# Softmax tiles copied into the split-operand type ahead of their transposes, in an LSH attention with two expert layers

## The chip, the core and the metric

The kernel runs on one core of a Trainium2 chip. The core has five engines with instruction streams of their own: PE (TensorE, matrix products; PEld are its weight loads), DVE (VectorE), ACT (ScalarE), POOL (GpSimd) and SP (SyncE, which here only issues DMAs). They wait for each other through semaphores. Each takes its own instructions in the order in which they stand. The metric is the device time of one execution in microseconds, as the median of three runs.

## The reference

Attention with hashed buckets over 2 batches, 8 heads, 768 positions and 64 dimensions: a query sees only the keys whose six projection signs are the same as its own. Two layers with a gate follow, 512 to 2048 to 512, over the 1536 tokens. All arrays are float32.

```python
q_bits = (np.einsum('bhsd,dk->bhsk', q, proj) > 0).astype(np.int64)
k_bits = (np.einsum('bhsd,dk->bhsk', k, proj) > 0).astype(np.int64)
...
mask = q_bucket[:, :, :, None] == k_bucket[:, :, None, :]
scores = scale * np.matmul(q, k.transpose(0, 1, 3, 2))
scores = np.where(mask, scores, -1000000000.0)
scores = scores - np.max(scores, axis=-1, keepdims=True)
attn = np.exp(scores)
attn = attn / (np.sum(attn, axis=-1, keepdims=True) + 1e-09)
return np.matmul(attn, v).astype(np.float32)
...
g = h * np.tanh(sp)        # layer 1, sp = softplus(h), h = x @ w_in
return (g @ w_out).astype(np.float32)
...
g = h - np.tanh(h)         # layer 2
return (g @ w_out).astype(np.float32)
```

## The kernel before

**Types.** A float32 value is split into a high and a low part, both held in fp32r, the type in which PE multiplies; a product is then two or three matmuls (high by high, high by low, low by high). Names that end in h and l are such parts. ACT or POOL makes the high part by a copy into fp32r, DVE or POOL the low part by a subtraction.

**Attention.** The eight pairs of heads (two heads share a pair, `g` counts pairs, `h` the head in it) run one after the other. For a pair, `load` fetches q, k and v; `halves_split` splits q and k in halves of 384 positions; `piece` takes the projection signs; `stack` copies the parts into four stacked operands a, b, c and d by eight DMAs per head (`b<-kh` twice, `a<-qh`, `a<-ql`, `d<-kl`, `c<-qh`, `d<-z`, `c<-z`). Then the queries go in tiles of 128, three tiles to a half, two halves to a head. `scores` (L566) makes one tile: four matmuls (L582, L583) into PSUM, a clamp on DVE that also takes the row's extreme (L586), and Exp on ACT (L609) into the tile p with the row sums beside it. `chunk` (L631) works on a half: for each of its six column blocks PE transposes the three p tiles (L643, three transposes per chunk, 576 in all), the 128x384 result is split into ph and pl, and a later `product` (L617) multiplies both with the values (L622, L623). For most chunks ACT copies and DVE subtracts (L659, L662); for the "pooled" ones of `POOL_C` ACT copies to f (L651) and POOL does both parts (L375, L655). `gather` (L669) joins the halves of the output; `inverse` (L681) adds, inverts and transposes the row sums and spreads them over the partitions by way of DRAM (four stores, two loads); `finish` (L710) multiplies and splits the result into xh and xl.

**Layers.** From about 235 us on the two layers run on PE with products by blocks (L1023 to L1025, L1100, L1101, L1113, L1338). They start from xh and xl and are not touched by the change.

**What sets the order.** Nothing is issued where the code stands. `op` records each operation with an engine, a cost and a key (a due time); `Plan.order` then plays the recorded operations through, picks for each engine the one that can start first (the lower key where several can), with costs and latencies from the table of constants at the head of the file, and emits the instructions in that order. So a change of the constants moves instructions on every engine. Each tile name has a ring of buffers: p has six (`P_BUFS`), and a new tile waits until the one whose buffer it takes has been read for the last time. All DMAs but a few at the start are issued by SP, in one queue.

## Time and profile before

| | |
|---|---|
| median of 3 runs | 741.01 us (741.01 to 741.36) |
| profiled execution | 740.89 us, span 739.1 us from the first to the last instruction |
| busy over the span | PE 98%, PEld 91%, DVE 87%, ACT 72%, POOL 24% |
| stretch of 60 to 220 us (attention) | PE 159.85 of 160 us, ACT 155.31, DVE 148.24, POOL 133.85, DMA share 0.66 |
| granted clock | 1.00 in every stretch of the attention, 0.999 over the span |

Averages over the span mix the attention, in which all engines work, with the layers, in which POOL has nothing to do. So the stretches are read apart. A matmul's busy time is modelled to its end, and matmuls overlap: a transpose is shown with 272 ns, though transposes start 109 ns apart. A busy PE is therefore not yet a full one; what a matmul costs is read from the distance between starts.

### The profile page before, as it was taken

How to read it: one execution, taken by the hardware profiler on the slowest of the kernel's cores; microseconds unless marked ns; L12 is line 12 of the kernel's file. 1: busy time of each engine (PE TensorE's matmuls, PEld its weight loads, DVE VectorE, ACT ScalarE, POOL GpSimd, SP SyncE). 2: the span in 40 equal slices, each digit the busy share in tenths (PEclk: the TensorE clock that was granted, in tenths of full speed). 3: DMA queues.
4: the chain of work that ended last, by engine and by line, in shares of the span. 5: the costliest groups of instructions: out<-in, count | busy, mean ns of one | idle time of the engine just before them, and what ended most of it. 6: DMA issues, size and time to landing. Idle time of an engine off the chain costs nothing.

```text
span 739.1 us, 13094 instructions
## 1 busy us (share of the span) xinstructions
PE 727.7 (98%) x4382; PEld 673.6 (91%) x4382; DVE 643.8 (87%) x1372; ACT 529.7 (72%) x1140; POOL 179.7 (24%) x224
## 2 busy tenths in 40 slices
PE   7999999999999999999999999999999999999998
PEld 4889999999999999999999999998998899999997
DVE  6988998998999999999898899789898775767893
ACT  6989999999997866767676676666565445466660
POOL 5677987988961000000000000000000000000000
PEclk9999999999999999999999999999999999999999
DMA  7775775785562655545655567999986786735621
GB/s 215 184 200 130 204 201 129 204 211 126 156 175 88 231 197 168 172 156 179 204 181 186 185 232 247 330 330 329 350 295 251 270 278 232 244 144 186 222 87 64
DMA packets 59390, 150.96 MB, mean 204 GB/s; under 512 B 7990, under 2 KB 20406, under 8 KB 59324
## 3 DMA queue, kind: packets, MB, share of 16 engines
q1 hardware_dynamic: 58892, 149.65, 63.9%
q8 instruction: 34, 0.56, 0.3%
q10 hardware_dynamic: 432, 0.49, 0.2%
q14 instruction: 32, 0.26, 0.1%
HBM read 88.18 MB, written 43.04 MB: 178 GB/s over the span
## 4 chain that ended last, share of the span: by engine, by line
PE 93%; DVE 2%; DMA 2%; ACT 2%; issue 1%; POOL 0%; ACTq 0%; SPq 0%; DVEq 0%; POOLq 0%
PE pt L1023 11%; PE pt L1025 11%; PE pt L1024 11%; PE pt L643 8%; PE pt L1101 6%; PE pt L1113 6%; PE s L1100 6%; PE pt L1100 6%; PE pt L1338 5%; PE s L582 4%; PE pt L622 4%; PE pt L623 4%; PE s L583 4%; PE s L1338 3%; PE s L1113 3%; DVE p L586 1%
## 5 line engine op out<-in xcount | busy, mean ns | idle before, releaser
L1023 PE MATMUL pt<-xh,a 128*128 128x384 f32 x288 | 96.7, 336 | 0.0
L1025 PE MATMUL pt<-xh,a 128*128 128x384 f32 x288 | 96.7, 336 | 0.0
L1024 PE MATMUL pt<-xl,a 128*128 128x384 f32 x288 | 96.6, 335 | 0.0
L586 DVE TENSOR_SCALAR_CACHE_REDUCE p<-s 128x768 f32<-128x768 f32 x93 | 88.2, 948 | 7.6 <-PE s L583 5.7
L609 ACT ACTIVATE p<-p,mn 128x768 f32<-128x768 f32 x96 | 90.7, 945 | 3.1 <-DVE p L586 2.0
L662 DVE TENSOR_TENSOR pl<-pt,ph 128x384 fp32r<-128x384 f32 x148 | 78.5, 546 | 8.6 <-ACT ph L659 7.6
L643 PE MATMUL pt<-cst,p 128*128 128x128 f32 x576 | 83.8, 272 | 1.1 <-DVE pl L662 1.1
L643 PEld LDWEIGHTS pt<-cst,p 128*128 128x128 f32 x576 | 69.5, 140 | 6.1 <-DVE pl L662 1.4
L659 ACT CAST ph<-pt 128x384 fp32r<-128x384 f32 x148 | 68.8, 484 | 5.2 <-PE pt L622 3.1
L1101 PE MATMUL pt<-gh,o 128*128 128x256 f32 x256 | 71.7, 280 | 0.0
L622 PE MATMUL pt<-ph,vt 128*128 128x384 f32 x192 | 70.4, 367 | 0.3 <-ACT f L651 0.2
L582 PE MATMUL s<-b,a 128*128 128x512 f32 (+1 forms) x186 | 68.2, 367 | 1.1 <-DVE p L586 0.7
L623 PE MATMUL pt<-pl,vt 128*128 128x384 f32 x192 | 64.9, 338 | 0.4 <-DVE pl L662 0.4
L583 PE MATMUL s<-d,c 77*128 77x512 f32 (+3 forms) x186 | 59.3, 340 | 0.6 <-ACT raw L846 0.6
L802 DVE TENSOR_TENSOR gl<-pl,gh 128x384 fp32r<-128x384 f32 x96 | 52.4, 551 | 6.5 <-ACT gh L1047 6.5
L1023 PEld LDWEIGHTS pt<-xh,a 128*128 128x128 f32 x288 | 54.1, 188 | 3.3 <-ACT pl L1042 0.2
L1024 PEld LDWEIGHTS pt<-xl,a 128*128 128x128 f32 x288 | 54.1, 188 | 1.3
L1025 PEld LDWEIGHTS pt<-xh,a 128*128 128x128 f32 x288 | 54.1, 188 | 0.1
L1047 ACT CAST gh<-pl 128x384 fp32r<-128x384 f32 x96 | 48.7, 514 | 2.1 <-DVE pl L802 1.1
L1101 PEld LDWEIGHTS pt<-gh,o 128*128 128x128 f32 x256 | 48.3, 189 | 0.0
L1061 ACT COPY ph<-pt 128x384 f32<-128x384 f32 x56 | 26.9, 481 | 28.7 <-PE pt L1025 28.6
L1100 PE MATMUL pt<-gh,o 128*128 128x512 f32 x128 | 47.2, 391 | 0.0
(301 smaller groups left out, 2080.7 us busy)
## 6 DMA issues: line engine op xcount, KB each, us to landing
w<-w SPq DMA_DIRECT2D x52, 512.0 KB
raw<-in_moe_w_in_dram SPq DMA_DIRECT2D x32, 512.0 KB
raw<-in_moe_w_out_dram SPq DMA_DIRECT2D x32, 512.0 KB
split<-a SPq DMA_DIRECT2D x24, 512.0 KB
a<-split SPq DMA_DIRECT2D x24, 512.0 KB
w<-t SPq DMA_DIRECT2D x32, 256.0 KB
o<-split SPq DMA_DIRECT2D x24, 256.0 KB
b<-kh SPq DMA_DIRECT2D x30, 192.0 KB
```

Of the source, the lines that this page charges most:

```text
L582: nc.tensor.matmul(o, a()[:, tok], b_()[:, kc], start=True, stop=False)
L583: nc.tensor.matmul(o, c_()[used, tok], d_()[used, kc], start=False, stop=True)
L586: nc.vector.tensor_scalar(out=out, in0=in_, scalar1=MASKED, scalar2=None, op0=ALU.min, op1=ALU.min, accum_out=low)
L609: lambda: nc.scalar.activation(out=p(), in_=p(), func=AF.Exp, bias=mn(), scale=-1.0, accum_out=sm()[:, h, t:t + 1],),
L622: nc.tensor.matmul(o()[:, :HB], vt()[:, c, :], ph()[:, :HB], start=(c == 0), stop=False)
L623: nc.tensor.matmul(o()[:, :HB], vt()[:, c, :], pl()[:, :HB], start=False, stop=(c == NT - 1))
L643: nc.tensor.transpose(pt()[:, t * P:(t + 1) * P], ps[t]()[:, c * P:(c + 1) * P], ident)
L1023: nc.tensor.matmul(o, tl()[:, 0, c], at_(0, kk), start=start and kk == 0, stop=False, skip_group_check=not start)
L1024: nc.tensor.matmul(o, tl()[:, 0, c], at_(1, kk), start=False, stop=False, skip_group_check=not start)
L1025: nc.tensor.matmul(o, tl()[:, 1, c], at_(0, kk), start=False, stop=kk == 1, skip_group_check=not start)
L1100: nc.tensor.matmul(a()[:, n, :], w()[:, y, c], flat[x][:, :SEG], start=st, stop=sp)
L1101: nc.tensor.matmul(r()[:, 0, rest], w()[:, y, c], flat[x][:, SEG:], start=st and d % 2 == 0, stop=sp, skip_group_check=True)
```

## The change

- **Moved tiles.** Of the three p tiles of a half, the first (`MOVED`) is copied after Exp by a DMA, bit by bit, into a second p tile of type fp32r (128x768, 393 KB). Its six transposes read the copy and write in fp32r; those of the other two tiles stay in float32. That makes 32 copies, and 192 of the 576 transposes. The identity is now held in fp32r, made by one POOL copy at the start.
- **Eight p buffers** instead of six, for tiles and copies alike.
- **q** is scaled where it is split: ACT's copy into qh carries the factor, and DVE makes ql from the unscaled q. Before, for pairs 1 to 7, ACT scaled q in place, then copied it, and POOL made ql.
- **Pooled chunks**: in both halves of a head c = 1 and 4, instead of 1 and 4 in the first and 4 in the second. The last pair stays as it was.
- **Row sums**: one `inverse` per pair for both halves (pairs 0 to 6) instead of two; `finish` of both halves then comes after the second. The r buffers hold both halves.
- **Constants** of the planner: lookahead of the scores 9 to 12 ticks, of the products 4 to 5 chunks, latencies, rates and due times. So the order on all engines is new.
- **Start**: the constants land in a buffer of the weights, two columns are loaded a second time by a DMA on ACT's queue; seven filling matmuls (L495) instead of three.

```diff
-POOL_C = ((1, 4), (4,))
+POOL_C = ((1, 4), (1, 4))
-SPLIT_S = (1, 3, 5)
+SPLIT_S = (1, 2, 4)
-T_BUFS, P_BUFS, U_BUFS = 4, 6, 3
+T_BUFS, P_BUFS, U_BUFS = 4, 8, 3
+MOVED = ((0,), (0,))
+MOVE_KEY = 12.8
...
-AHEAD = 9
-PV_LAG = 4
+AHEAD = 12
+PV_LAG = 5
...
@@ halves_split
-            if nm == "q" and g:
-                if Q_SCALE == "ACT":
-                    op("ACT", 0.42, k0 - 0.1, lambda c=c: nc.scalar.activation(out=raw()[:, c], in_=raw()[:, c], func=AF.Copy, scale=-SCALE), [], [(raw, i)])
...
-                op("ACT", 0.42, k0, lambda c=c: nc.scalar.copy(th()[:, c], raw()[:, c]), [(raw, i)], [(th, i)])
-            elif nm == "q":
+            if nm == "q":
...
-            if nm == "q" and not g:
+            if nm == "q":
@@ scores
+        if t in MOVED[half]:
+            pr = buf("p", "p", [P, S], F32R)
+            dma(P * S * 4, key + MOVE_KEY, lambda: pr().bitcast(F32), p, [p], [pr], rate=FAST)
+            return pr
         return p
@@ chunk
             for t in ts:
-                nc.tensor.transpose(pt()[:, t * P:(t + 1) * P], ps[t]()[:, c * P:(c + 1) * P], ident)
-
-        op("PE", 0.327, key, lambda: transpose(range(TB)), ps, [(pt, 0), (pt, 1)])
+                o, x = pt()[:, t * P:(t + 1) * P], ps[t]()[:, c * P:(c + 1) * P]
+                if t in MOVED[half]:
+                    nc.tensor.transpose(o.bitcast(F32R), x, ident)
+                else:
+                    nc.tensor.transpose(o, x, ident.bitcast(F32))
+
+        op("PE", 0.327 - 0.049 * len(MOVED[half]), key, lambda: transpose(range(TB)), ps, [(pt, 0), (pt, 1)])
@@ inverse (of one half before, of a list of halves after)
-            lambda: nc.vector.tensor_tensor(out=used(), in0=sm(), in1=tiny, op=ALU.add),
+            lambda: nc.vector.tensor_tensor(out=used(), in0=sm()[:, :, i0:i0 + nh], in1=tiny[:, :, :nh], op=ALU.add),
...
-                nc.sync.dma_start(out=r()[h * D:(h + 1) * D], in_=d[h:h + 1].to_broadcast([D, HB]))
+                nc.sync.dma_start(out=r()[h * D:(h + 1) * D, i0 * HB:(i0 + nh) * HB], in_=d[h:h + 1].to_broadcast([D, nh * HB]))
@@ loop over the pairs
-                if h == 1:
-                    inverse(g, half, at(NT * n - 2))
+                if h == 1 and (half or g == len(pairs) - 1):
+                    inverse(g, (half,) if g == len(pairs) - 1 else (0, 1), at(NT * n - 2))
...
-                    if h == 1:
+                    if h == 1 and g == len(pairs) - 1:
                         finish(g, half, u, key + 0.3)
+                    elif h == 1 and half:
+                        for i in range(2):
+                            finish(g, i, us[i], key + 0.3 + i)
@@ start
-    nc.scalar.dma_start(out=cst, in_=cst_d)
+    nc.scalar.dma_start(out=land[:, 0, 0:P + 66], in_=cst_d)
+    nc.scalar.dma_start(out=cst[:, 0:2], in_=cst_d[:, P:P + 2])
```

Two places show what the change moves. On PE, in the middle of the attention, before (cst holds the identity; L582 and L583 are the scores, L622 and L623 the products with the values, L643 the transposes):

```order
L643 MATMUL pt<-cst,p 128x128 x3
L622 MATMUL pt<-ph,vt 128x384
L623 MATMUL pt<-pl,vt 128x384
L622 MATMUL pt<-ph,vt 128x384
L623 MATMUL pt<-pl,vt 128x384
L582 MATMUL s<-b,a 128x512
L583 MATMUL s<-d,c 128x512
L582 MATMUL s<-b,a 128x256
L583 MATMUL s<-d,c 128x256
L643 MATMUL pt<-cst,p 128x128 x6
```

The same engine and stage after the change (L642 is the transpose of the copy, L644 that of the other two tiles, L619 and L620 are the products, L575 and L576 the scores):

```order
L642 MATMUL pt<-ident,p 128x128
L644 MATMUL pt<-ident,p 128x128 x2
L619 MATMUL pt<-ph,vt 128x384
L620 MATMUL pt<-pl,vt 128x384
L575 MATMUL s<-b,a 128x512
L576 MATMUL s<-d,c 128x512
L575 MATMUL s<-b,a 128x256
L576 MATMUL s<-d,c 128x256
L642 MATMUL pt<-ident,p 128x128
L644 MATMUL pt<-ident,p 128x128 x2
```

In each chunk the transpose of the copy now stands first, ahead of the two float32 ones; the kinds of the matmuls around it are the same.

On SP, around the stack copies for the first head of the third pair, before (L701 and L705 are the stores and the spread of the row sums):

```order
L701 DMA inv0_1_142<-rt_809 6x32 x4
L381 DMA raw_915<-in_moe_w_out_dram 128x512
L381 DMA k_943<-in_k_dram 128x768
L705 DMA r_973<-inv0_1_142 64x384 x2
L381 DMA b_994<-kh_822 64x768 x2
L381 DMA a_1013<-qh_897 64x768
L381 DMA a_1013<-ql_996 64x768
L381 DMA d_1044<-kl_882 64x768
L381 DMA c_1054<-qh_897 64x768
L381 DMA d_1044<-z_927 13x768
```

and after (`p_888<-p_756` and its like are the copies of the moved tiles; L705 and L709 are the stores and the spread):

```order
L705 DMA inv0_0_142<-rt_818 12x32 x4
L384 DMA p_888<-p_756 128x768
L384 DMA w32_1_0_0_151<-w0_329 128x1024
L384 DMA p_928<-p_896 128x768
L709 DMA r_938<-inv0_0_142 64x768 x2
L384 DMA b_960<-kh_833 64x768 x2
L384 DMA a_990<-qh_894 64x768
L384 DMA a_990<-ql_915 64x768
L384 DMA d_1017<-kl_869 64x768
L384 DMA c_1028<-qh_894 64x768
L384 DMA p_1041<-p_996 128x768
L384 DMA d_1017<-z_906 13x768
```

Four copies per pair have joined the queue; one of them stands right behind the five stack copies of a head.

## Rows read from the trace of the kernel before

**Rows 1.** The page: busy time and share of the span, then one costly group.

```profile
PE 727.7 (98%) x4382; PEld 673.6 (91%) x4382; DVE 643.8 (87%) x1372; ACT 529.7 (72%) x1140; POOL 179.7 (24%) x224
...
L643 PEld LDWEIGHTS pt<-cst,p 128*128 128x128 f32 x576 | 69.5, 140 | 6.1 <-DVE pl L662 1.4
```

**Rows 2.** Stretches: length, busy time of each engine (instructions), clock, DMA share, GB/s.

```profile
0.00:20.00 20.00, 15.07 (x63) 10.36 (x63) 13.68 (x36) 13.53 (x26) 12.11 (x22) 1.00 0.80 221
...
400.00:500.00 100.00, 100.00 (x579) 93.64 (x578) 88.82 (x181) 67.72 (x139) 0.00 (x0) 1.00 0.73 253
...
60.00:220.00 160.00, 159.85 (x1056) 146.99 (x1054) 148.24 (x331) 155.31 (x346) 133.85 (x164) 1.00 0.66 171
```

**Rows 3.** PE's groups by form, 60 to 220 us: count | busy, mean ns.

```profile
L643 PE MATMUL pt<-cst,p 128*128 128x128 f32 x423 | 61.4, 272 | 0.0
L622 PE MATMUL pt<-ph,vt 128*128 128x384 f32 x142 | 51.8, 364 | 0.0
...
L582 PE MATMUL s<-b,a 128*128 128x512 f32 x71 | 32.3, 455 | 0.1
...
L582 PE MATMUL s<-b,a 128*128 128x256 f32 x71 | 20.0, 282 | 0.0
...
L478 PE MATMUL pt<-qh,pjh 128*64 128x384 f32 x10 | 3.6, 356 | 0.0
```

**Rows 4.** PE in order of time: start, length, instruction; distances between starts count.

```profile
100.77 0.34 PE L622 MATMUL pt<-ph,vt 128*128 128x384 f32 x1
...
101.47 0.82 PE L643 MATMUL pt<-cst,p 128*128 128x128 f32 x6
...
59.84 0.40 PE L583 MATMUL s<-d,c 77*128 77x512 f32 x1
...
60.07 0.28 PE L582 MATMUL s<-b,a 128*128 128x256 f32 x1
...
60.19 0.28 PE L583 MATMUL s<-d,c 77*128 77x256 f32 x1
```

**Rows 5.** Weight loads in order of time, three transposes after a wait.

```profile
25.17 0.31 PEld L643 LDWEIGHTS pt<-cst,p 128*128 128x128 f32 x3 [0.16 <-ACT z L461]
```

**Rows 6.** Timeline: last scores matmul of a tile, and its Exp.

```profile
66.73 0.28 PE L583 MATMUL s<-d,c 77*128 77x256 f32 x1
...
68.41 0.95 ACT L609 ACTIVATE p<-p,mn 128x768 f32<-128x768 f32 x1
```

**Rows 7.** Timeline: stack copies issued by SP, and POOL waiting for them.

```profile
65.47 1.18 SPq L381 DMA_DIRECT2D b<-kh  x2
...
70.47 0.99 POOL L375 TENSOR_SCALAR kh<-k 128x384 fp32r<-128x384 f32 x2 [0.64 <-DMA b<-kh]
```

**Rows 8.** Stretches with full DMA engines: stack copies, then loads from memory; last two columns.

```profile
110.00:112.50 2.50, 2.50 (x18) 2.24 (x17) 2.50 (x6) 2.25 (x6) 2.50 (x3) 1.00 1.02 200
...
104.00:105.50 1.50, 1.50 (x12) 1.41 (x11) 1.50 (x5) 1.50 (x4) 1.50 (x3) 1.00 0.98 367
```

**Rows 9.** Groups of ACT, DVE and POOL by form, 60 to 220 us.

```profile
L423 ACT ACTIVATE q<-q 128x384 f32<-128x384 f32 x10 | 5.5, 550 | 0.0
...
L662 DVE TENSOR_TENSOR pl<-pt,ph 128x384 fp32r<-128x384 f32 x108 | 57.2, 546 | 5.4 <-ACT ph L659 4.7
...
L691 DVE TENSOR_TENSOR rd<-sums,tiny 128x6 f32<-128x6 f32 x12 | 2.7, 228 | 0.0
...
L655 POOL TENSOR_TENSOR pl<-f,ph 128x384 fp32r<-128x384 f32 x35 | 36.5, 1042 | 1.9
L375 POOL TENSOR_SCALAR ph<-f 128x384 fp32r<-128x384 f32 x35 | 18.2, 520 | 17.3 <-ACT f L651 14.3 <-PE pt L623 2.0 <-PE pt L643 0.5
...
L454 POOL TENSOR_TENSOR ql<-q,qh 128x384 fp32r<-128x384 f32 x10 | 10.1, 1018 | 0.0
```

**Rows 10.** Timeline of the start: the q load's issue on ACT's queue, and PE's wait.

```profile
1.20 0.90 ACTq L408 DMA_DIRECT2D q<-in_q_dram  x2
...
16.30 0.39 PE L480 MATMUL pt<-kl,pjh 128*64 128x384 f32 x1 [1.47 <-POOL kl L454]
```

More of the change, by code (lines that the diff above doesn't have):

```diff
@@ L56 @@
 TOKS = ("DVE", 0.47)
-EPS = 0.0
+EPS = 0.14
 SLOW = 0.9
@@ L105 @@
 TOK_T = 3.0
-CONV_A = 10
+CONV_A = 0
 CONV_S = 24
@@ L369, in tile_lsh_attention_moe @@
     hot = plan.pools["f"].tile([P, XB], F32R, tag="f", name="hot")
+    land = plan.pools["w32"].tile([P, 2, DM], F32, tag="w3", name="land")
+    pj = land[:, 0, P + 2:P + 66]
     def x_tok(which, kk, t0, n):
@@ L572, in scores @@
         p, mn = buf("p", "p", [P, S]), buf("small", "mn", [P, 1])
-        sm = sums[g, half]
+        sm = sums[g]
         rows = (False, True) if g or h else (False, True, "bits")
@@ L679, in gather, with inverse @@
         )
-    def inverse(g, half, key):
-        sm, rd, rt = sums[g, half], rds[half], buf("rt", "rt", [P, 32])
-        tok = ("rd", half)
-        r = rs[g, half] = buf("r", "r", [P, HB])
-        n = 2 * TB
-        d = scratch.tile([2, HB], F32, name=f"inv{g}_{half}")
-        used = lambda: rd[:, :n].rearrange("p (h t) -> p h t", h=2)
+    def inverse(g, halves, key):
+        rt = buf("rt", "rt", [P, 32])
+        i0, nh = halves[0], len(halves)
+        rd, n = rds[i0], nh * 2 * TB
+        tok = ("rd", i0)
+        if (g, "r") not in rs:
+            rs[g, "r"] = buf("r", "r", [P, S])
+        r, sm = rs[g, "r"], sums[g]
+        d = scratch.tile([2, nh * HB], F32, name=f"inv{g}_{i0}")
+        used = lambda: rd[:, :n].rearrange("p (h i t) -> p h i t", h=2, i=nh)
         op(
             "DVE", 0.15, key,
-            lambda: nc.vector.tensor_tensor(out=used(), in0=sm(), in1=tiny, op=ALU.add),
-            [(sm, h, t) for h in range(2) for t in range(TB)], [tok],
+            lambda: nc.vector.tensor_tensor(out=used(), in0=sm()[:, :, i0:i0 + nh], in1=tiny[:, :, :nh], op=ALU.add),
+            [(sm, h, i, t) for h in range(2) for i in halves for t in range(TB)], [tok],
         )
@@ L704, in spread @@
             for h in range(2):
-                nc.sync.dma_start(out=r()[h * D:(h + 1) * D], in_=d[h:h + 1].to_broadcast([D, HB]))
-        op("DMA", C_STORE, key + 0.3, store, [rt], [("inv", g, half)])
-        op("DMA", C_SPREAD, key + 0.4, spread, [("inv", g, half)], [r])
+                nc.sync.dma_start(out=r()[h * D:(h + 1) * D, i0 * HB:(i0 + nh) * HB], in_=d[h:h + 1].to_broadcast([D, nh * HB]))
+        op("DMA", C_STORE, key + 0.3, store, [rt], [("inv", g, i0)])
+        op("DMA", C_SPREAD, key + 0.4, spread, [("inv", g, i0)], [(r, i) for i in halves])
     def finish(g, half, u, key):
         b, hp = pairs[g]
-        r = rs[g, half]
+        r = rs[g, "r"]
         t0 = b * NT + half * TB
@@ L718, in finish @@
         op(
-            eng, cost, key + 0.2, lambda: e.tensor_tensor(out=u(), in0=u(), in1=r(), op=ALU.mult),
-            [r], [(u, 0), (u, 1)],
+            eng, cost, key + 0.2, lambda: e.tensor_tensor(out=u(), in0=u(), in1=r()[:, half * HB:(half + 1) * HB], op=ALU.mult),
+            [(r, half)], [(u, 0), (u, 1)],
         )
@@ L734, in tile_lsh_attention_moe @@
             clear_stack()
+            op("POOL", 0.25, 6.0, lambda: pool_copy(ident, land[:, 0, 0:P]))
         else:
```

51 lines of the change are left out of this document (22 added, 29 removed).

## The prediction, made before the changed kernel was run

> **What bounds the kernel now.** I read the busy shares first, then the stretches, then how full PE is. PE is busy 98% of the span [rows 1]. In the layers it is busy 100 of 100 us, in the attention 159.85 of 160 us, with the clock at 1.00, which is the 2.4 GHz level; only the start has holes [rows 2]. But busy time is modelled, so I count instead what PE issues. Distances between starts give the price of a matmul [rows 4]: four products of 384 columns stand between 100.77 and 101.47, 0.175 us each; 512 columns take 0.23 (59.84 to 60.07), 256 take 0.12. Six transposes cover 0.82 us with the last one's modelled 0.272 in it, so they start 0.109 apart [rows 3, 4]. Between 60 and 220 us there are 423 transposes (46.1 us), 350 matmuls of 384 columns (L622, as many of L623, six groups of ten like L478, six of the layers: 61.3), 142 of 512 (L582, and as many of L583: 32.7) and 141 of 256 (16.9) [rows 3]. The sum is 157.0 us of 160. So PE is full to 98% and nothing else ends a wait for long: what PE saves there shortens the kernel, as long as the other engines and the DMAs keep up.
>
> **Transposes.** A float32 transpose costs 0.109 us. No transpose of an fp32r tile is in the trace. The bounds: no gain, if transposing sets the pace and not the type (0.109); and the pace of fp32r matmuls, 0.175 x 128/384 = 0.058. The nearest row is the second, since the fp32r matmuls go through the same array. The next transpose's weight load must be done by then: three loads after a wait cover 0.31 us [rows 5], one lasts 0.140 [rows 1], so their two distances sum to 0.17 where twice 0.109 would be 0.218; the first load thus freed the way after 0.06. I take 0.060. The copy's own fp32r load stands under the matmul ahead of it, which lasts 0.109 or more. That is 192 x 0.049 = 9.4 us off PE's path (bounds 0 and 9.8).
>
> The load is where the Trainium skill speaks against this change: the page "TensorE: Matmul & The Clock Gate", section "LDWEIGHTS (loading the stationary operand)", gives a load the number of its columns over 1.2 GHz, 107 ns for 128 columns. By that rule the second transpose would wait for its load whatever the first one costs, and the gain would be nil; the 0.06 worked out above speaks against the rule for these loads. The same page, section "Back-to-back issue gap", has about 81 ns for a sustained stream of loads and 128-column matmuls; by it the sum would be 192 x 0.028 = 5.4 us.
>
> **Copies.** Each of 32 moves 393 KB from SBUF to SBUF. Its DMA time lies between 1.07 us (367 GB/s, loads) and 1.97 (200 GB/s, the stack copies) [rows 8]. All 128 partitions move, as in the loads, so I take 1.2; the sum is 34 to 63 us on top of 0.66 of the time, a DMA share of 0.82 to 0.95 over the attention's some 215 us. What counts is when a copy lands. The last scores matmul of a tile is through at 66.85 (start and 0.12), its Exp at 69.36, 2.5 us later [rows 6]. A stack copy behind others lands 4.4 us after its issue: the second b starts at about 66.06 and POOL gets its go at 70.47 [rows 7]; a copy has twice the bytes, so 2.5 + 4.4 + 0.5 to 1.0 = 7.4 to 7.9 us in a bad spot. In the new order the PE work between a moved tile's scores and its first transpose, counted with the prices above, is 6.2 to 11.6 us after the first tile, 8.4 in the middle; ten tiles have under 7.6. If a copy is late, PE stands at its transpose, and the products and the next scores queued behind it with it, and so ACT's casts and DVE's clamps. Waits of 0 to 1 us for those ten: none to 5 us, and I take 1.6, since most copies don't stand behind a batch.
>
> SP waits for Exp before it issues a copy, and behind that stand the stack copies and the row sums' spread; they are due a head later, so 1 to 2 us there cost nothing. Against that 28 stores and 14 spreads of the row sums go from the queue.
>
> **The other engines**, for the 160 us of rows 2, which PE would do in 152.4. DVE: two chunk subtractions fewer per pair (12 x 0.55), two splits of q more (10 x 0.55), six times three short operations on the sums fewer (0.6 each, the first 0.23) [rows 9]: 144 us, 94%. POOL: 12 pooled chunks more at 1.56, ten ql fewer at 1.02 [rows 9]: 142 us, 93%. ACT: ten scalings fewer at 0.55 [rows 9]: 150 us, 98%. None is over PE, so these edits cost and bring nothing by themselves; with ACT the cover is thin. That both halves are finished together puts six POOL operations in a row of work; the products of a pooled chunk, which would wait, lag by five chunks, some 5 us, where POOL needs 1.56.
>
> **Start.** The second constant load goes ahead of the q load on ACT's queue: about 0.4 us, the length of such an issue (half of 0.90) [rows 10]. PE waits until 16.30 anyway for kl of the second pair [rows 10]; the first tile's copy must land by about 18, which it may miss by little. Four more filling matmuls (0.7 us) lie in the wait before the scores. I take 0.4, bounds -0.5 and 2.
>
> **Layers.** The order of PE is nearly unchanged there, and PE is full [rows 2]; what the attention saves stays saved. I see nothing that would be late next at the passage.
>
> **Sum**, against the profiled execution's 740.9 (its span 739.1 and 1.8 around it; 0.1 under the median of 741.0): -9.4 + 1.6 + 0.4 gives **733.5**. With the bounds of copies and start, and with the 3 us of holes in the stretch filled in part by the longer lookahead, its own range is 729.5 to 737.
>
> **Rivals.** (1) *The fp32r transposes are no cheaper*, since the second transpose of a chunk waits 0.109 for its load, or the array's transposing sets the pace. For it: no row shows one. Against: the 0.06 between two loads [rows 5]. Time: 740.9 + 0.4 + 0.5 for a few late copies = 741.8. The rule on loads of the Trainium skill ("TensorE: Matmul & The Clock Gate", "LDWEIGHTS (loading the stationary operand)") would have it so. (2) *Copies land late*: PE then stands before most moved tiles. For it: the stack copies' 200 GB/s, a queue in order, a DMA share that may reach 0.95. Against: most distances of 8 us and more. If the landing takes 6.5 us from Exp's end, so 9.0 from the scores, the missing parts of all 32 distances sum to 27 us; a wait also gives time to the tile behind, so half of it counts, 14 us: 740.9 - 9.0 + 14 = 746, slower. It decides from about 6 us between Exp and landing. (3) *ACT becomes the bound*: where it can't go over today's 97%, the stretch takes 150/0.971 = 154.3 us and not 152.4, over 215 us 2.5 more: 736. For it: its 155.31 of 160. Against: ACT's waits can hide in modelled ends as PE's do.
>
> **How the numbers follow.** Forecast 0.65, rival (1) 0.11, (2) 0.14, (3) 0.10. The range 729.5 to 742 takes in the forecast, (1) and (3), and leaves out (2). A measurement can tell about 0.2%, 1.5 us, from no change. Faster by more: the forecast, (3), and a little of (1), where the pitch lies between its bounds: 0.77. Within: most of (1) and a little of (2), 0.08. Slower: the rest of (2), and (1) with late copies, 0.15.
>
> **What would show it.** In the changed profile, starts of a chunk's transposes 0.06, 0.109, 0.109 apart; if 0.109 throughout, rival (1). In PE's waits, few on the DMA of p, under 3 us in all; much more is rival (2). The last transpose of the attention some 7 us earlier, and the layers as long as now. ACT waiting for nothing while PE waits for ph is rival (3). What would make the prediction wrong most easily is the landing of the copies: it rests on one row of a smaller DMA.

## The result, and the profile of the changed kernel

The changed kernel takes 751.81 us (751.01 to 755.66, four runs) where the kernel before takes 741.18 us: a ratio of 1.015, 95% interval 1.0111 to 1.0188. It is slower by 1.5%, where 733.5 us and a gain had been forecast. The profiled execution shown here took 755.66 us, with a span of 752.3; it is the longest of the four. The medians below leave out two executions, one of e6 and one of e17, that took 1457 and 3504 us.

Stretches of the changed kernel (columns as in [rows 2]):

```profile
0.00:20.00 20.00, 13.61 (x44) 9.13 (x44) 12.03 (x31) 8.78 (x15) 8.17 (x17) 1.00 0.69 188
15.00:20.00 5.00, 2.93 (x14) 1.36 (x12) 4.94 (x15) 2.90 (x5) 3.02 (x4) 1.00 1.06 242
20.00:27.00 7.00, 6.16 (x27) 5.67 (x27) 4.18 (x11) 6.52 (x15) 5.90 (x8) 0.51 0.62 200
...
36.00:40.00 4.00, 1.46 (x11) 0.91 (x9) 2.66 (x6) 2.48 (x7) 2.60 (x3) 1.00 0.77 191
40.00:44.20 4.20, 4.20 (x21) 3.88 (x19) 1.44 (x3) 2.82 (x6) 2.82 (x3) 0.59 0.66 221
...
60.00:220.00 160.00, 154.01 (x1016) 133.33 (x1016) 145.45 (x300) 147.13 (x324) 140.38 (x176) 1.00 0.84 223
400.00:500.00 100.00, 100.00 (x579) 93.77 (x578) 89.32 (x179) 66.83 (x133) 0.00 (x0) 1.00 0.70 238
```

Three things differ from [rows 2]. PE has holes in the attention, 154.01 busy of 160 us where it was 159.85. The start has longer ones (13.61 busy of the first 20 us for 15.07). Behind the stretches 15 to 20 and 36 to 40, in which PE does little (2.93 of 5 us, 1.46 of 4), the granted clock falls to 0.51 and 0.59, the 1.2 GHz level. The layers are as they were: 579 matmuls in 400 to 500 us in both.

Busy time is modelled, so PE is counted here as the prediction did it, instructions between 60 and 220 us times the distance of their starts. Before, that gave 157 of 160 us. The changed kernel has 271 float32 transposes (0.109), 136 of copies (0.06), 333 matmuls of 384 columns (0.175), 138 of 512 (0.23) and 138 of 256 (0.119): 144 us, 90%. PE now stands still for 16 of these 160 us.

What it waits for, from 60 to 240 us (engine, line, what it waited for: us in total, times, the longest; a PE wait and the PEld wait of the same place overlap):

```profile
PE s L575 <- DVE p L579: 3.6, 8, 0.6
PE pt L642 <- DMA p<-p: 1.8, 2, 1.2
```

```profile
PEld s L575 <- DVE p L579: 11.2, 27, 1.0
```

The first line of the PE waits and the PEld line are one place: the scores of a tile (L575) can't start before VectorE's clamp (L579) has read the tile before out of PSUM, since there is one scores buffer `s`. The same place in the kernel before:

```profile
PEld s L582 <- DVE p L586: 2.0, 8, 0.3
```

It went from 2.0 to 11.2 us. Waits on copies are the smaller part.

The transposes themselves do what was forecast. PE in order of time (start, length, instruction):

```profile
101.28 0.23 PE L642 MATMUL pt<-ident,p 128*128 128x128 f32 x1
101.34 0.38 PE L644 MATMUL pt<-ident,p 128*128 128x128 f32 x2
101.48 0.42 PE L619 MATMUL pt<-ph,vt 128*128 128x384 f32 x1
101.74 0.34 PE L620 MATMUL pt<-pl,vt 128*128 128x384 f32 x1
```

The transpose of the copy frees the way after 0.06 us. From the first transpose to the second product it is 0.46 us; less one product of 0.175 the three transposes take 0.285. That is the median over the chunks of 60 to 220 us too; counted in the same way, three float32 transposes took 0.331 before. So PE has 192 x 0.046 = 8.8 us less to do, about 9, and yet the kernel is 10.6 us longer.

### The profile page after: what moved, and what is told of

It is laid out like the page before. It is cut to its first block, busy times and chain, and to the rows that moved or that the text cites. A ratio compares the mean times of both kernels' runs of the same rounds, so it can differ in the third digit from the quotient of the medians.

```text
span 752.3 us, 13159 instructions
## 1 busy us (share of the span) xinstructions
PE 731.4 (97%) x4386; PEld 668.4 (89%) x4386; DVE 650.1 (86%) x1351; ACT 526.5 (70%) x1126; POOL 188.4 (25%) x239
## 4 chain that ended last, share of the span: by engine, by line
PE 81%; DVE 5%; DMA 4%; issue 3%; POOL 3%; ACT 2%; SPq 0%; ACTq 0%; DVEq 0%; POOLq 0%
PE pt L1031 10%; PE pt L1033 10%; PE pt L1032 10%; PE pt L1121 6%; PE s L1108 6%; PE pt L1109 6%; PE pt L1108 5%; PE pt L1346 5%; PE s L575 3%; PE pt L644 3%; PE s L1346 3%; PE s L1121 3%; PE s L576 3%; PE pt L619 3%; PE pt L620 3%
## 5 line engine op out<-in xcount | busy, mean ns | idle before, releaser
L579 DVE TENSOR_SCALAR_CACHE_REDUCE p<-s 128x768 f32<-128x768 f32 x93 | 88.4, 950 | 16.3 <-PE s L576 15.0
L663 DVE TENSOR_TENSOR pl<-pt,ph 128x384 fp32r<-128x384 f32 x134 | 71.7, 548 | 6.2 <-ACT ph L660 5.5
L619 PE MATMUL pt<-ph,vt 128*128 128x384 f32 x192 | 75.4, 393 | 0.6 <-ACT z L454 0.4
L575 PE MATMUL s<-b,a 128*128 128x512 f32 (+1 forms) x186 | 69.8, 375 | 4.3 <-DVE p L579 3.9
L644 PE MATMUL pt<-ident,p 128*128 128x128 f32 x384 | 71.0, 279 | 0.0
L660 ACT CAST ph<-pt 128x384 fp32r<-128x384 f32 x134 | 63.6, 482 | 6.0 <-PE pt L619 3.1
L620 PE MATMUL pt<-pl,vt 128*128 128x384 f32 x192 | 66.0, 344 | 1.2 <-POOL pl L656 0.7
L576 PE MATMUL s<-d,c 77*128 77x512 f32 (+3 forms) x186 | 60.5, 346 | 1.1 <-ACT c L454 1.1
L656 POOL TENSOR_TENSOR pl<-f,ph 128x384 fp32r<-128x384 f32 x58 | 60.5, 1043 | 1.3
L575 PEld LDWEIGHTS s<-b,a 128*128 128x128 f32 x186 | 35.6, 192 | 18.6 <-DVE p L579 12.1
L642 PE MATMUL pt<-ident,p 128*128 128x128 f32 x192 | 46.7, 248 | 3.7 <-DMA p<-p 3.6
```

What stands on the lines that cost most here:

```text
L575: nc.tensor.matmul(o, a()[:, tok], b_()[:, kc], start=True, stop=False)
L576: nc.tensor.matmul(o, c_()[used, tok], d_()[used, kc], start=False, stop=True)
L579: nc.vector.tensor_scalar(out=out, in0=in_, scalar1=MASKED, scalar2=None, op0=ALU.min, op1=ALU.min, accum_out=low)
L619: nc.tensor.matmul(o()[:, :HB], vt()[:, c, :], ph()[:, :HB], start=(c == 0), stop=False)
L620: nc.tensor.matmul(o()[:, :HB], vt()[:, c, :], pl()[:, :HB], start=False, stop=(c == NT - 1))
L644: nc.tensor.transpose(o, x, ident.bitcast(F32))
```

## The loop that sets the pace

The timelines show why PE waits. First the kernel before, where the scores of [rows 6] begin at 66.03 and the last of them starts at 66.73:

```profile
67.05 0.96 DVE L586 TENSOR_SCALAR_CACHE_REDUCE p<-s 128x768 f32<-128x768 f32 x1
...
68.16 0.51 PE L582 MATMUL s<-b,a 128*128 128x512 f32 x1
```

The clamp begins 0.20 us after the scores are through (66.85), lasts 0.96, and the next scores start 0.15 us later: one turn of 2.13 us. Now a turn of the changed kernel:

```profile
142.01 2.12 DVE L437 SCALAR_TENSOR_TENSOR ql<-q,qh 128x384 fp32r<-128x384 f32 x2
...
142.13 0.50 PE L575 MATMUL s<-b,a 128*128 128x512 f32 x1 [0.31 <-DVE p L579]
...
142.83 0.29 PE L576 MATMUL s<-d,c 77*128 77x256 f32 x1
...
144.06 0.94 DVE L579 TENSOR_SCALAR_CACHE_REDUCE p<-s 128x768 f32<-128x768 f32 x1
...
145.06 0.50 PE L575 MATMUL s<-b,a 128*128 128x512 f32 x1 [0.55 <-DVE p L579]
```

The scores are through at 142.95, but VectorE is in two splits of q until 144.06; PE runs out of other work at about 144.5 and stands until the clamp has ended: 2.93 us for the turn. The two splits take 2.12 us together, where a split takes 0.56 in the median. The second one lasts until GpSimd has ended this instruction, at 143.72, and 0.41 us more:

```profile
142.53 1.19 POOL L552 TENSOR_TENSOR vt<-v,vt 128x384 fp32r<-128x384 f32 x1
```

More of this is shown at e13.

Counted over all clamps of 60 to 220 us, the shortest turn in any kernel here is 1.92 us (scores 0.70 to 0.80, 0.20 to the clamp, clamp 0.95, 0.06 to the next scores). The mean turn was 2.29 us before: 0.29 from scores to clamp, 0.27 from the clamp to the next scores. In the changed kernel it is 2.33: 0.41 and 0.19. Cheaper transposes shorten only the last of these, PE's other work after the clamp has ended; what holds VectorE when the scores are ready lengthens the first. The table below has the mean turn for each experiment. As all tiles go through one buffer, the turns add up to the stretch: the mean turn is the pace itself, and only its parts can tell what slowed it.

## The experiments

"Turn" is that mean; "PE filled" is counted as above; "clamp wait" is the PEld line for the scores from 60 to 240 us. Ratios are to runs of the kernel before on the same chip. A difference between two experiments on different chips is given by these ratios too. e2, e3, e4, e6, e9 and e10 stand in the text alone. Line numbers in the rows are those of each kernel's own code.

| run | us, median | ratio (95%) | PE filled | turn, us | clamp wait, us |
|---|---|---|---|---|---|
| before | 741.2 | 1 | 98% | 2.29 | 2.0 |
| changed | 751.8 | 1.015 (1.0111 to 1.0188) | 90% | 2.33 | 11.2 |
| e1 changed, no copies | 748.8 | 1.0108 (1.0091 to 1.0125) | 91% | 2.31 | 12.5 |
| e14 e1, one constant load | 744.8 | 1.0048 (1.0033 to 1.0063) | 91% | 2.32 | 12.3 |
| e16 e14, float32 transposes | 746.2 | 1.0063 (1.0044 to 1.0083) | 95% | 2.32 | 7.5 |
| e17 e14, q split twice | 757.7 | 1.0213 (1.0195 to 1.0231) | 86% | 2.45 | 17.7 |
| e18 e14, q split off VectorE | 748.8 | 1.0082 (1.0057 to 1.0107) | 90% | 2.35 | 12.4 |
| e5 before, cheap transposes, no copies | 738.9 | 0.9955 (0.9932 to 0.9978) | 95% | 2.26 | 5.4 |
| e11 e5, less work on ScalarE | 738.2 | 0.9946 (0.9922 to 0.9970) | 95% | 2.25 | 5.4 |
| e12 e5 with the copies | 754.0 | 1.0169 (1.0146 to 1.0191) | 89% | 2.38 | 6.0 |
| e7 before, all planner constants | 749.9 | 1.0105 (1.0055 to 1.0155) | 94% | 2.37 | 9.6 |
| e8 before, leads alone | 754.4 | 1.0169 (1.0152 to 1.0185) | 93% | 2.39 | 8.0 |
| e15 before, latencies alone | 758.2 | 1.0221 (1.0183 to 1.0260) | 94% | 2.36 | 7.6 |
| e13 before, one price 0.320 for 0.327 | 759.8 | 1.0273 (1.0231 to 1.0314) | 90% | 2.46 | 12.1 |

### Copies and start, in the changed kernel's own order

**e1, no copies.** The planner still plans the copies, so every order stays; only the DMAs go.

```diff
-                out=p(), in_=p(), func=AF.Exp, bias=mn(), scale=-1.0,
+                out=(pr or p)(), in_=p(), func=AF.Exp, bias=mn(), scale=-1.0,
...
-            dma(P * S * 4, key + MOVE_KEY, lambda: pr().bitcast(F32), p, [p], [pr], rate=FAST)
+            op("DMA", max(ISSUE, P * S * 4 / FAST), key + MOVE_KEY, lambda: None, [p], [pr])
```

> The changed kernel with every engine's order as it is, but without the 64 copies: the Exp of a moved tile writes the split-operand type straight into the buffer that the copy would have filled, and the transposes read that at once. (What is computed differs in one thing: a third of the softmax values are rounded to that type.) Changed kernel 751.0. Theory A, the copies land late and cost it the gain: the transposes' 9 us stay and the waits go, so 751 - 14 or more, 733 to 738. Theory B, the loss comes from the other edits and the order that they give (PE waits for DVE's clamp, DVE for PE, ACT for the pooled chunks, the start): only the three long waits of the transposes on a copy go, 2.1 + 0.8 + 1.3 = 4.2 us, so 746 to 748, still slower than the kernel before (741.2).

Measured: 748.82 us (747.97 to 748.98), 3.0 less. The copies that went are 32, not the 64 of the expectation. Theory A falls: with no copy left, the loss is still 8 us. In the profiled runs most of what the copies cost is one place, seen in the changed kernel's chain of waits (start, length, what), where the copy issued at 31.10 lands at 39.31:

```profile
31.10 8.21 DMA p<-p
...
112.08 7.13 DMA p<-p
```

PE stands for it, after other holes since 36 us:

```profile
39.45 0.25 PE L642 MATMUL pt<-ident,p 128*128 128x128 f32 x1 [1.84 <-DMA p<-p]
```

Then it runs at 0.59 of the clock until 44.2. In e1 that hole is gone and the clock stays up:

```profile
36.00:40.00 4.00, 4.00 (x30) 3.79 (x29) 3.77 (x9) 3.95 (x10) 2.17 (x3) 1.00 0.64 215
40.00:60.00 20.00, 19.57 (x129) 16.85 (x128) 18.90 (x40) 18.53 (x43) 17.74 (x22) 1.00 0.72 175
60.00:220.00 160.00, 155.44 (x1027) 134.85 (x1026) 145.67 (x304) 147.98 (x326) 140.05 (x175) 1.00 0.68 168
```

From 60 to 220 us PE is hardly better off than with the copies (155.44 for 154.01).

**e2, float32 transposes with the copies.**

```diff
-                    nc.tensor.transpose(o.bitcast(F32R), x, ident)
+                    nc.tensor.transpose(o, x.bitcast(F32), ident.bitcast(F32))
```

> The changed kernel with its order and its copies, but the transposes of the copied tiles run in float32, at the old price (192 x 0.047 = 9.0 us more work for PE). If PE is the bound of 60 to 220 us and only the copies hold it up (theory A), nearly the whole of it shows: 758 to 760. If PE there waits for the other engines in any case (theory B), much of it falls into those waits: 752 to 756. If the transposes are no cheaper in the split type: 751.

Measured: 753.46 us (751.73 to 756.66; ratio 1.0178, 1.0150 to 1.0206). Nine microseconds more work on PE cost 1.7 us by the medians, within the scatter. PE is not the bound there, as far as the scatter allows.

**e3, one constant load.**

```diff
-    nc.scalar.dma_start(out=cst[:, 0:2], in_=cst_d[:, P:P + 2])
+    nc.vector.tensor_copy(cst[:, 0:2], land[:, 0, P:P + 2])
```

> The changed kernel without its second constant load (128 rows of 8 bytes) on ACT's queue, ahead of the first q load; VectorE takes the two columns out of the first load instead. If that load is why the q load took 6.13 us (3.56 before): the q load lands 2 to 2.6 us earlier, and PE's hole before 20 us shrinks by as much; with the clock at full speed through 20 to 27 us another 3.4 us comes back: 745.5 to 749. If the clock's fall has another cause: 748.5. If the q load is late for its place in the queue: 751.

Measured: 751.13 us, but 746.86 to 755.67 from run to run (ratio 1.0143, 1.0094 to 1.0191): by itself not resolved. In its profiled run the first chunk's ph came 3.5 us earlier than in the changed kernel; at the 60th ph it was 4.9 us ahead, at the 73rd, 16 us on, only 0.4. In between one short VectorE instruction, which takes 0.15 to 1.04 us in the changed kernel, lasted as long as GpSimd worked without a pause (until 101.38), and the clamp behind it came late:

```profile
97.42 3.99 DVE L695 TENSOR_TENSOR rd<-sums,tiny 128x12 f32<-128x12 f32 x1
...
103.10 0.80 PE L575 MATMUL s<-b,a 128*128 128x512 f32 x1 [3.30 <-DVE p L579]
```

Behind this hole the granted clock was 0.67 in 100 to 105 us and 0.64 in 105 to 110.

**e14, both together**: the edits of e1 and e3.

> The changed kernel's order without copies (748.8) and also without the second constant load, which brought the first chunk 3.5 us earlier in the profiled run of its own test but was lost to the copies later. If start and copies add up: 744 to 746. If the start's gain is taken back at VectorE's clamp: 748.

Measured: 744.84 us (743.66 to 744.93), 4.0 below e1 without overlap of the runs (4.4 by the ratios). In the profiled runs e14 is 5.2 us ahead of e1 at the first chunk's ph and 5.1 at the last. So, without the copies, the second constant load costs 4 us, all of it at the start; with the copies in place (e3) its cost is not resolved. How so small a load costs that much stands in the timeline of the changed kernel's start (the last column of the ACT line is the wait):

```profile
1.18 0.46 ACTq L1415 DMA_DIRECT2D cst<-cst_dram  x1
1.66 0.43 SPq L384 DMA_DIRECT2D v<-in_v_dram  x1
1.70 0.90 ACTq L411 DMA_DIRECT2D q<-in_q_dram  x2
...
7.85 0.52 ACT L427 ACTIVATE qh<-q 128x384 fp32r<-128x384 f32 x1 [4.90 <-DMA q<-in_q_dram]
```

In [rows 10] the q load goes at 1.20, ahead of SP's v load in the kernel before:

```profile
1.64 0.43 SPq L381 DMA_DIRECT2D v<-in_v_dram  x1
```

The second constant load shifts the q load by 0.5 us, as forecast, and so behind the v load. By the chains of waits it then lands 6.13 us after its issue (3.56 before, 3.50 in e14), and PE's first product waits for it. With e14 the clock too is at full speed through the start:

```profile
0.00:20.00 20.00, 14.96 (x68) 10.55 (x69) 14.16 (x40) 12.61 (x24) 11.20 (x21) 1.00 0.85 235
20.00:40.00 20.00, 18.50 (x126) 16.27 (x125) 18.42 (x40) 19.02 (x42) 15.95 (x19) 1.00 0.70 169
```

That the v load ahead of it delays the q load is inferred from the order of the issues; it was not tested by itself.

### What the 9 us of PE are worth

**e16**: e14 with the edit of e2.

> The run without copies and with one constant load (744.8) again, every order the same, but the transposes of tiles 0 and 3 in float32: 9.0 us more work for PE, nothing else. What the cheap transposes are worth when no copy is in the way. If PE is the bound there: 753 to 754. If PE waits for VectorE's clamp and the rest in any case, as it does for 16 us of 60 to 240: 746 to 749.

Measured: 746.15 us (745.93 to 747.43), 1.3 us above e14. By the ratios, each to the kernel before on its own chip, it is 1.1, and at most 3.7 from the low end of one interval to the high end of the other. PE has 9 us more to do and the kernel grows by little; the mean turn is 2.32 us in both. The clamp wait falls from 12.3 to 7.5 us:

```profile
PEld s L575 <- DVE p L579: 7.5, 19, 1.0
```

So more than half of the work that was saved turned into waits for the clamp. The parts of the turn say the same: with cheap transposes (e14) the clamp is followed by the next scores 0.17 us later and not 0.23, but it begins 0.42 us behind the scores and not 0.39. This settles the main point: PE's own work does not set the pace of this order; the turn of scores and clamp does.

**e5**: the kernel before with every order as it was, Exp of the first tile of each half writing fp32r into a buffer of its own, transposes reading it (as in e1; the planner's prices unchanged). For this the identity is held in fp32r, by one POOL copy more, and the constants land in a buffer of the weights, loaded once.

> The kernel before with every engine's order as it is, but the Exp of tiles 0 and 3 writes the split-operand type into a buffer of its own and their transposes read it: the cheap transposes without any copy. (What is computed differs in one thing: a third of the softmax values are rounded to that type.) If PE is the bound of this order, as the counted starts said (157.0 of 160): 741 - 9 = 732, and not above 734. Theory C, the other engines wait for each other as soon as PE is faster: 736 to 739.

Measured: 738.88 us (737.26 to 742.01, ten runs), ratio 0.9955 (0.9932 to 0.9978): 2.5 us less by the medians, 1.6 to 5.0 by the interval, and not the 9. In the order of before, too, PE falls back from 98% to 95% filled and waits:

```profile
PEld s L589 <- DVE p L593: 5.4, 18, 0.5
```

From the clamp to the next scores it is 0.20 us where it was 0.27, but from the scores to the clamp 0.34 where it was 0.29: what PE saves in the one part, VectorE takes in part in the other. Of the versions that do all the work it is the one that beats both kernels. It does so at the price of rounding a third of the softmax values.

**e11**: e5 with ScalarE's scaling of q left out (`lambda: None` in its place).

> The run with the cheap transposes and no copies in the order of before (738.9), every order kept, but ScalarE's scaling of q left out from the second pair on (22 operations of 0.55 us, 5.5 us of them in 60 to 220 us; q stays unscaled there, and the scores with it). If ScalarE, 156 of 160 us busy, is what keeps the 9 us of the transposes from showing: 732 to 735. If PE or the waits between the engines are: 738 to 739.

Measured: 738.18 us (737.58 to 740.12), 0.7 below e5, with overlap. The order has 14 such operations (ten of them in the stretch), not 22 as the expectation says: 7.7 us less for ScalarE bring 0.7 by the medians, 0.7 by the ratios. ScalarE is not the bound; rival (3) falls.

### The order by itself

None of these four changes the work, but for four filling matmuls more at the start of e7; they change numbers from which the order is made.

**e7**: the sixteen changed planner constants in the kernel before.

```diff
-AHEAD = 9
+AHEAD = 12
-PV_LAG = 4
+PV_LAG = 5
...
-FIRST = (0.0, 1.0, 2.0, 6.0)
+FIRST = (1.0, 0.0, 2.0, 6.0)
```

> The kernel before with the sixteen constants of the planner from the changed kernel alone (lead of the scores 12 for 9 ticks, lag of the products 5 for 4, start, stack, values, load, q first of the loads, latencies, seven filling products): no edit of the work itself. If the new order is the cause of the loss: 748 or more. If the edits of the work are (q split on VectorE, more pooled chunks, row sums together): 740 to 743.

Measured: 749.90 us (749.6 to 750.65). The new order alone costs 8.5 us by the medians (4 to 11 by the interval).

**e8**: five of them, the leads (`AHEAD`, `PV_LAG`, `STACK`, `VALUES`, `LOAD`).

> The kernel before (741) with five constants of the planner alone: scores 12 ticks ahead instead of 9, products 5 chunks behind instead of 4, stack 16 for 12, values 14 for 11, load 16 for 15. All sixteen constants gave 749.9. If the longer leads are the cause (more tiles under way at once, PE's scores then wait for VectorE's clamp): 747 or more. If the cause is the start or the latencies: 740 to 743.

Measured: 754.35 us (753.92 to 754.86).

**e15**: three others (`EPS`, `LATE`, `LATG`), leads as before.

> The kernel before with the planner's tolerance and two latencies of the changed kernel (0.14 for 0; 0.31 for 0.22; 0.4 for 0.5), leads and work as before. If the longer leads are the fault: 740 to 743. If any other order than that of before costs: 746 to 756, as with the leads alone (754.4).

Measured: 758.20 us (753.2 to 760.12). Leads and latencies each cost more than all sixteen together, so no one constant is the culprit.

**e13**: one price that no engine executes.

```diff
-        op("PE", 0.327, key, lambda: transpose(range(TB)), ps, [(pt, 0), (pt, 1)])
+        op("PE", 0.32, key, lambda: transpose(range(TB)), ps, [(pt, 0), (pt, 1)])
```

> The kernel before with one number changed that no engine executes: the planner's price of a chunk's three transposes, 0.320 us for 0.327. The same work comes out in another order on every engine. If the order of the kernel before is a rare good one, and any other costs: 746 to 756, with the waits of PE's scores on VectorE's clamp well over the 2.0 us of before. If a new order by itself is harmless and the longer leads are the fault: 740 to 743.

Measured: 759.79 us (756.68 to 764.12): 18.7 us for nothing but another order of the same work. Its clamp wait, and that of e7:

```profile
PEld s L582 <- DVE p L586: 12.1, 25, 3.0
```

```profile
PEld s L582 <- DVE p L586: 9.6, 19, 1.2
```

No order planned anew here reached that of the kernel before, with its mean turn of 2.29 us; those that are counted have 2.31 to 2.46. The changed kernel's, freed of copies and second load (e14), gives the lowest time of these.

The traces show a part of what differs between the orders. The wait of 3.0 us in e13's row looks like this (VectorE, GpSimd, PE):

```profile
112.11 3.60 DVE L830 TENSOR_SCALAR w<-raw 128x512 uint32<-128x512 uint32 x1
...
114.44 0.98 POOL L726 TENSOR_TENSOR xl<-u,xh 128x384 fp32r<-128x384 f32 x1
...
116.64 0.80 PE L582 MATMUL s<-b,a 128*128 128x512 f32 x1 [2.58 <-DVE p L586]
```

The first instruction takes 0.42 us in the median. Here GpSimd works without a pause from before its start until 115.42; it ends 0.29 us after that, the clamp comes behind it, PE stands, and the granted clock is 0.76 from 116 to 123 us. Added up over 0 to 240 us, what VectorE's instructions last beyond the median of their kind (counting those that are over 0.1 us longer) is 4.1 us before, 11.5 in e7, 13.7 in e8, 8.1 in e15, 10.5 in e13, 9.5 in the changed kernel and 7.7 in e14. So which VectorE instruction meets which of GpSimd is one thing that the order decides. How much of the 8 to 19 us it makes was not tested by a run.

**e6**: the changed kernel with `MOVED = ((), ())`, planned anew.

> The changed kernel with no tile moved, all transposes in float32, no copies, planned anew: the other edits alone. Theory B: they are slower than the kernel before by themselves, by 753.5 (its order with dear transposes) less the 3.0 us of the copies about 750. Theory A: 741, as before.

Measured: 748.60 us (746.60 to 750.47); ratio 1.0092 (1.0063 to 1.0121). The other edits and their order cost 7 us without any moved tile, as theory B had it. Four of these are the second constant load, if e14's figure holds here as well, which no run shows.

### The copies in a tight order

**e4, e9, e10** plan the move anew in the kernel before: e4 the move alone (copy due 12.8 after the scores), e9 the same with the copy due at 3.0, e10 with 6.0 and the longer leads of e8.

> The kernel before (741) with the copies and the cheap transposes of tiles 0 and 3 alone, eight slots for both kinds, one constant load, the identity copied to the split type; none of the other edits (q scaled as before, row sums of each half, one half's pooled chunks, the planner's constants of before). Theory A, the copies are what cost the gain: 741 - 9 + 14 or more, 745 and slower. Theory B, the loss is in the other edits and their order: the gain of 9 us less the 3.0 us that leaving the copies out brought in the changed kernel, 735. Theory C, PE waits for the other engines in this order too, so that 9 us less work brings little (it was worth 2.5 us in the changed kernel): 738 to 742.

> The move alone in the kernel before, as in the run that gave 760.4, but with the copies ranked right behind the Exp (key 3.0 instead of 12.8, which with scores only 9 ticks ahead lies behind the transposes' own). If the 19 us there came from the copies' rank on SP's queue: 738 to 745. If they come from the short lead (score to transpose 10 us, score to landing 5.3 to 10.9 in the changed kernel): 755 or more.

> The kernel before with the move (key 6.0) and the five longer leads. If the copies need the lead and nothing else is wrong with it: 735 to 741. If the lead itself costs what the sixteen constants cost, and the copies 3 us more: 748 to 752, as the changed kernel.

Measured: 760.45 (760.1 to 763.6), 754.87 (754.08 to 755.97) and 755.33 us (752.84 to 756.46). They agree with theory A on their face, but e13 shows that planning anew costs as much without a copy, so they tell copies and order not apart.

**e12** does: e5's order, with each copy issued by hand right behind its Exp.

```diff
+            if p.pr:
+                nc.sync.dma_start(out=p.pr().bitcast(F32), in_=p())
```

> The kernel before with every engine's order as it is, and the 64 copies put in by hand, each issued on SP's queue right behind its Exp, their transposes in the split type: the run with 738.9 plus the copies, nothing planned anew. If the copies' flight of 2.6 to 8.2 us doesn't fit the 10 us that this order leaves between scores and transposes: 748 or more, with PE's waits on the copies in the rows. If it fits, and the 755 to 760 of the planned versions came from the planning: 739 to 743.

Measured: 753.96 us (751.15 to 755.04), 15 us above e5 with nothing else changed (the copies are 32 here too). Who waits, from 0 to 240 us, PEld and then POOL:

```profile
PEld pt L486 <- POOL kl L460: 8.2, 7, 2.4
PEld s L589 <- DVE p L593: 7.2, 20, 0.7
PEld pt L653 <- DMA p<-p: 6.8, 6, 2.1
```

```profile
POOL kl L460 <- DMA d<-kl: 12.7, 7, 4.1
```

Some half of it is rival (2) as written, PE before a transpose whose copy hasn't landed (6.8 us). Most of the rest is a wait that the prediction had priced at nothing: POOL can't overwrite kl until the stack copies `d<-kl` have landed (12.7 us; 0.6 in e5), and PE's projection of kl waits for POOL (8.2; 1.3 in e5). That the new copies delay the stack copies follows from the edit, which changes nothing else; whether by SP's queue or by the DMA engines that they share was not taken apart.

### VectorE's share

**e17**: e14 with each half's split of q run twice from the second pair on.

```diff
-                    lambda c=c: nc.vector.scalar_tensor_tensor(
+                    lambda c=c: [nc.vector.scalar_tensor_tensor(
...
-                    ),
+                    ) for _ in range(2 if g else 1)],
```

> The run without copies and with one constant load (744.8) again, but each half's split of q on VectorE (from the second pair on) runs twice in a row, writing the same values: 14 operations of 0.55 to 0.75 us more, 8 to 10 us of VectorE's time. If VectorE stands in the way of PE's scores, so that the q split that the change put there costs PE time: 749 to 754, and the split itself as much. If it falls into VectorE's idle time, as forecast: 745 to 746.

Measured: 757.68 us (757.09 to 758.04), 12.8 above e14, 12.2 by the ratios. Fourteen operations more, in the stretch as follows:

```profile
L437 DVE SCALAR_TENSOR_TENSOR ql<-q,qh 128x384 fp32r<-128x384 f32 x20 | 15.6, 789 | 0.4
```

So 14 x 0.79 = 11 us of VectorE's time come out as 12 to 13 us of the kernel, though VectorE is busy for only 146 of 160 us: what it does ahead of a clamp goes straight into the loop (the scores wait 0.55 us for their clamp here, 0.42 in e14). A part is the clock, granted at 0.96 in 20 to 40 us where e14 has 1.00.

**e18**: e14 with q scaled and copied by ScalarE and its low part made by GpSimd, as before the change, at the same places of the order.

> The run without copies and with one constant load (744.8) again, PE's and SP's orders the same, but q from the second pair on is scaled and split as in the kernel before: scaled in place and copied by ScalarE (14 operations of 0.55 us more), its low part by GpSimd (14 of 1.02 us more), and VectorE is rid of 14 operations of 0.55 to 0.75 us. Doubling these on VectorE cost 13.0 us. If the split on VectorE was the wrong place for it: 733 to 740, faster than the kernel before. If GpSimd (137 of 160 us busy) or ScalarE (148 of 160) becomes the bound instead: 744 to 750.

Measured: 748.78 us (747.56 to 748.95), 3.9 above e14, 2.5 by the ratios, with intervals that touch. VectorE has less to do (138.96 for 146.63 us) and the kernel is no faster. Counted chunk by chunk from the timelines, its profiled run is behind e14's by 2 us at the first chunk, 3.4 at 79 us and 5.2 at the end; most of it thus comes early, with the clock at 0.91 in 20 to 40 us:

```profile
20.00:40.00 20.00, 18.32 (x114) 15.92 (x113) 15.62 (x36) 18.73 (x41) 15.11 (x19) 0.91 0.60 145
```

So the place of the q split, VectorE or ScalarE and GpSimd, is not what the changed kernel loses by: it got none of the 733 to 740. Doubling a piece of work and taking it away need not be mirror images: where it is taken away, here, two other engines get it.

## Why the prediction was wrong, step by step

- **"What PE saves there shortens the kernel."** This step failed, and it is the main one. PE was indeed filled to 98%, but it is tied in a turn with VectorE through the one scores buffer. Of a mean turn of 2.29 us PE's own work after the clamp is only 0.27; when that shrinks, the clamp itself comes later behind the scores, since VectorE is busy with other work (0.29 to 0.34 us in e5). Filled to 98% by its own work, PE looked like the bound; with 9 us less work the kernel gave back 1.3 us (e16) and 2.5 (e5). The prediction compared engines by their sums over 160 us, and none was over PE; it did not follow the chain scores, clamp, next scores through the one buffer.
- **The new order** had no term in the sum. The prediction priced the instructions that move only by the distance from scores to transposes. e7, e8, e13 and e15 put its price at 8 to 19 us for the same work. e14 has the changed kernel's order without copies and without the second load: 3.8 us over before with 9 us less for PE; with PE's transposes as before (e16) it is 4.0 us by the medians and 4.7 by the ratio, the other edits included.
- **Copies**, forecast at 1.6 us (0 to 5): 3.0 in the changed kernel (e1), within the bounds. PE's waits on the copies come to 3.6 us where the sign of being right was under 3. The flight was read well, 7.4 to 7.9 us in a bad spot against 8.21 and 7.13 from issue to landing in the two worst. What was missed is that a hole also costs clock. "1 to 2 us there cost nothing", said of the stack copies behind them on SP, failed in the tight order (e12).
- **Start**, forecast at 0.4 us (-0.5 to 2): 4.0 (e14 against e1), a term mis-sized tenfold. The issue took the 0.5 us that were forecast; that the q load then lands 6.13 us after its issue and not 3.56, and that the clock falls after the hole, was not seen.
- **Transposes**: right. 0.06 for the first and less work as forecast, 8.8 us for 9.4. Rival (1) falls. With it falls, for these loads, the rule of the Trainium skill ("TensorE: Matmul & The Clock Gate", "LDWEIGHTS (loading the stationary operand)") that 128 columns take 107 ns to load: by that rule the second transpose would start 0.107 after the first, and it starts after 0.06.
- **Other edits cost nothing**: not shown for each. q on VectorE took 0.75 us in the mean in the stretch and not 0.55, since some of the splits last until a GpSimd instruction has ended; but it is no worse there than where it was (e18). The prediction added each engine's work by its usual lengths and had no term for VectorE's instructions lasting longer beside GpSimd's. The pooled chunks and the joint row sums were not taken apart, since any edit that is planned anew brings a new order with it.
- **Rivals.** (2) named the right sign, its time of 746 was too low, and its mechanism is 3 of the 10.6 us. (3) falls by e11. The rival that came true, that another engine's loop takes PE's gain and the new order costs on top, was not among them.
- **Layers**: right; the profiled run is 14.1 us behind that of before at 311 us and 13.2 at the end.

Of the 10.6 us, then, 7.0 go when the copies and the second constant load are both left out in place: 3.0 with the copies, then 4.0 with the load. In the other order the first step is not resolved (0.7 with e3, in a scatter of 9 us), so the sharing out between the two is less sure than their sum. The remaining 3.6 to 3.8 are the order together with the other edits, less the 1.3 that the transposes bring. What stays open is which pieces of that order matter. The mean turn can't say it, as it is the pace itself: in the profiled runs of e15, e8 and e13 it ranks as their own times do (2.36, 2.39 and 2.46 us for 753.2, 753.9 and 756.7). The longer VectorE instructions beside GpSimd's are the nearest piece, and no run tests them.

## What to carry to other kernels

An engine that is filled to 98% need not give back what is saved on it where it is tied in a loop with others: before pricing a saving, lay one turn of that loop out from the timeline (here scores, clamp, next scores through a single buffer), and ask which part of the turn the saving shortens and what another engine does in the part ahead of it. Where a planner makes the order, run the old work in the new order, or the new work in the old, before judging an edit; here a price changed from 0.327 to 0.320 cost more than any edit. And look for instructions that last longer than the others of their kind: they show two engines in each other's way. A short extra DMA at the start can cost far more than its own length: here 4.0 us for an issue of 0.5.

## What the runs showed of the hardware

**The clock fell in the middle of a busy kernel.** PE was busy 2.93 of 5 us from 15 to 20, and 1.46 of 4 from 36 to 40; behind each, the granted clock was at the 1.2 GHz level, 0.51 over 20 to 27 and 0.59 over 40 to 44.2, and full again after. The kernel before has 1.00 in all these stretches. At half speed the same matmuls take about twice as long (a product 0.32 us and not 0.175, at 41.04), so some 10 us at that level cost about 5 us of PE's time, an estimate from these rows. The Trainium skill ("TensorE: Matmul & The Clock Gate", "HAM oscillation — how this bites in real kernels") describes it for matmuls that wait for DMAs: the hole is paid a second time at the lower clock. The rows agree.

**Some VectorE instructions last until GpSimd has ended one of its own.** In 19 traces, from 0 to 240 us, 100 VectorE instructions lasted over 0.6 us longer than the median of their kind, up to 4.47 us for `rd<-sums` (e10) and 3.60 for `w<-raw` (e13). Each ended 0.01 to 0.55 us behind the end of a GpSimd instruction, nearly always by the same distance for its kind (0.28 to 0.29 for `w<-raw`, 0.02 to 0.03 for `rd<-sums`). All of them have their operands outside PSUM. The clamps, which read PSUM, never took more than 0.96 us (1751 of them), the subtractions into pl that read PSUM never more than 0.56 (2557). That GpSimd is the cause is read from these times; no run takes it away.

**The order is worth as much as the work.** Four kernels with the work of the kernel before, one of them with four more filling matmuls, took 750 to 760 us in other orders (e7, e8, e13, e15).
